# One group of PSUM transposes instead of two, and W1 and W2 in turn for groups 0 to 3, in a causal convolution with a low-rank mixer

## The chip, the core and the metric

The kernel runs on one core of a Trainium2 chip. Its time is the device time of one execution in microseconds (us). The engines are named as in the profile: PE (matrix products; PEld is its weight load), DVE and ACT (both move results out of PSUM), POOL (constants, copies inside SBUF, and the issue of transfers that convert f32 to bf16), SP (issue of other transfers).

## What is computed

Two stages on x of 8 batches, 4224 positions and 192 channels, all in f32 outside:

```python
# stage 1: causal convolution over 7 taps, 8 heads of 24 channels, taps softmaxed per head
w = softmax(weight)                                   # 8 x 7
y[b, s, h, :] = sum_k w[h, k] * x_pad[b, s + k, h, :] # 6 zeros ahead
# stage 2: mixer
h  = y.transpose(0, 2, 1) @ U @ V                     # U: 4224 x 32, V: 32 x 4224, over positions
u  = y + h.transpose(0, 2, 1)
ch = np.maximum(u @ w_ch1, 0.0) @ w_ch2               # 192 x 768 and 768 x 192
out = u + ch
```

h of a position needs the whole batch: first tt = Uᵀy (32 x 192 per batch), then V times tt.

## The kernel before

Positions are cut into tiles of 128: 33 per batch, 264 in all, in 33 groups of eight that run across batches. `manual_schedule` (line 43) means that every engine runs its instructions in the order in which the program writes them; nothing is reordered. Tiles come from pools; PSUM is one pool of eight banks of 512 f32 (line 54), and a new bank waits for the last reader of the tile that had its place.

For a batch the stages are: `conv` or `conv32` (products with a banded matrix made from the taps, evicted from PSUM as y in bf16), `tt_mm` (the products with U), `tt_split` (the sum as a high part by ACT and a low part, the difference, by DVE), `tt_sum` or `tt_done` (sum over four partial rows into tt_sb). For a group: `h_group` (V times tt, eight products, line 457, and additions on DVE that give u, line 479), `transp` (u transposed by a DMA from SP, line 498, as uT), `w1` (36 products in six row blocks of two banks each, line 554; each bank is evicted with relu by ACT or DVE, lines 568 and 570, chosen by a pattern such as "AD"), `w2` (four pairs of tiles, 12 products each, line 583; DVE adds u, line 592, and SP stores, line 600).

**The start.** x of batch 0 comes in three pieces (`KP`, line 86): 20 tiles, then 7, then 6. Line numbers of what happens until W1 starts: constants (109 to 230), warming products on zeros (`idle`, 151 to 161 and 280), the bands (`band_half`, 233), conv of the first piece (690), `u_layout` (694; it brings U, loaded four positions to a row, into tile order with the matrices Eq), U4 by POOL (701), and then the second and third piece with tt between them (735 to 739). The last piece's tt products (`tt_late`) use U4, four copies of U side by side, so that tt_sb follows without a further sum.

Groups 0 and 1 do not take the DMA transpose. `yT_part` multiplies y with the identity so that yᵀ lands in PSUM (line 509), and `hT_part` adds h in the same banks (line 524); ACT and DVE evict the sum as uT. These pieces are interleaved with the end of tt: some transposes run while DVE makes tt_sb.

**The order after that** is written out in `SLOTS` (line 619): a row has the groups of its W1, the groups of its W2, and what is done ahead of which tile pair of W2: "h3" is h and transpose of group 3, "d1" conv of batch 1, "t1" and "s1" its tt, "c2:0:3:AAD" conv of three heads of batch 2 with the eviction pattern AAD, "x2:6" copies on POOL for batch 2, "l2:2" a load of x held back behind the last W2. Groups 0 and 1 have their W1 ahead of both W2; W2 lags W1 by one group until group 3, and from then on three groups of W1 are followed by three of W2. `LOADS` (line 670) holds further loads of x back until a given row block of W1.

**Transfers from POOL** go out in program order, and each waits for the landing of the eighth before it.

Of the kernel before, what the change touches and what calls it, by code (L numbers as in the profile page):

```python
# [7 lines left out]
ALU = mybir.AluOpType  # L8
# [6 lines left out]
def kernel(  # L15
# [10 lines left out]
    nc = tc.nc  # L26
# [59 lines left out]
    KP = [{0: (0, 10), 1: (0, 10)}, {1: (10, NB1 // 2)}, {0: (10, NB0 // 2)}]  # L86
# [21 lines left out]

    dif = cst.tile([P, BW], F32, name="dif")
# [3 lines left out]
    fp = cst.tile([P, P], I32, name="fp")  # L113
    nc.gpsimd.iota(fp[:], pattern=[[1, P]], base=P, channel_multiplier=-1)
    efp = cst.tile([P, 4, P], F32, name="efp")
    iota(efp[:], [[-1, 4], [1, P]], 0, -4)
# [15 lines left out]
    V0_sb = cst.tile([R, 2 * GT * P], BF16, name="V0_sb")  # L132
    nc.gpsimd.dma_start(out=V0_sb[:], in_=moe_V[:, 0 : 2 * GT * P])
# [8 lines left out]
    zz = cst.tile([P, P], F32, name="zz")  # L142
    nc.vector.memzero(zz[:])  # L143

    rq = cst.tile([P, 2], F32, name="rq")
    for r in range(4):
        for n, v in enumerate((32.0, -128.0)):
            nc.vector.memset(rq[QB * r : QB * r + QB, n : n + 1], v * r)
    wps = bank()

    def idle(n, w=4):
        for _ in range(n):
            nc.tensor.matmul(  # L153
                out=wps[:, 0 : w * P].rearrange("p (n t) -> p n t", t=P),
                lhsT=zz[:],
                rhs=zz[:].unsqueeze(1).to_broadcast([P, w, P]),
                start=True,
                stop=True,
            )

    idle(4)


# [3 lines left out]
    for hh in range(2):  # L167
        nc.vector.memzero(bands[hh][:])
    x_zero(0, nc.vector)
    nc.vector.tensor_scalar(  # L170
        out=dif[:], in0=dif[:], scalar1=rq[:, 0:1], scalar2=None, op0=ALU.add
# [13 lines left out]
    nc.vector.tensor_tensor(  # L185
        out=hot[:],
        in0=dif[:].unsqueeze(1).to_broadcast([P, KC, BW]),
        in1=tap[:].unsqueeze(2).to_broadcast([P, KC, BW]),
        op=ALU.is_equal,
    )  # L190
    ident = cst.tile([P, P], BF16, name="ident")
    nc.vector.tensor_scalar(
        out=ident[:], in0=fp[:], scalar1=float(P), scalar2=None, op0=ALU.is_equal
# [15 lines left out]
    for hh in range(2):  # L209
# [10 lines left out]
    Eq = cst.tile([P, 4, P], BF16, name="Eq")  # L220
    nc.vector.tensor_scalar(
        out=Eq[:], in0=efp[:], scalar1=rq[:, 1:2], scalar2=None, op0=ALU.is_equal
    )

    nc.vector.tensor_scalar(
        out=fp[:], in0=fp[:], scalar1=R - 1, scalar2=None, op0=ALU.bitwise_and
    )
    R4 = cst.tile([P, P], BF16, name="R4")
    nc.vector.tensor_scalar(
        out=R4[:], in0=fp[:], scalar1=0.0, scalar2=None, op0=ALU.is_equal  # L230
    )

    def band_half(hh):
# [9 lines left out]
        for r in range(4):  # L243
            o = QB * (r % 2)
            evac(
                "AD"[hh],
                bands[hh][QB * r : QB * r + QB, :, o : o + BW],
                bp[QB * r : QB * r + QB, 0 : HQ * BW].rearrange("p (h t) -> p h t", h=HQ),
            )
# [10 lines left out]
    def u_layout(up):  # L260
        nb = [nfull + (1 if 32 * jj < nlast else 0) for jj in range(4)]
        for a in range(4):
            for jj in range(4):
                nc.tensor.matmul(
                    out=up[jj][:, 0 : nb[jj] * R],
                    lhsT=Eq[32 * jj : 32 * jj + 32, a, :],
# [11 lines left out]

    band_half(0)
    idle(1, 2)  # L280
    band_half(1)


# [112 lines left out]
    def tt_mm(b, js, p=None):  # L396
# [3 lines left out]
        for n, j in enumerate(js):  # L400
# [102 lines left out]
    def yT_part(g, parts):  # L503


        for c, i0, i1, p, _ in parts:
            for i in range(i0, i1):
                for hf in range(2):
                    nc.tensor.matmul(  # L509
                        out=p[HB * hf : HB * hf + HB, (i - i0) * P : (i - i0 + 1) * P],  # L510
                        lhsT=yt[0][:, GT * g + 4 * hf + i, HB * c : HB * c + HB],
                        rhs=ident[:],
                        start=(i == i0),
                        stop=False,
                        tile_position=(0, HB * hf),
                    )

    def hT_part(g, parts):

        uTt[g] = uts.tile([P, 4, 3, P], BF16, name="uT")  # L520
        for c, i0, i1, p, _ in parts:
            for hf in range(2):
                t0 = (2 * g + hf) * 4 * P
                nc.tensor.matmul(  # L524
                    out=p[HB * hf : HB * hf + HB, 0 : (i1 - i0) * P],
                    lhsT=ttb[0][0:R, HB * c : HB * c + HB],
                    rhs=V0_sb[:, t0 + i0 * P : t0 + i1 * P],
# [4 lines left out]
        for c, i0, i1, p, eng in parts:  # L532
            evac(
                eng,
                uTt[g][:, i0:i1, c, :],
                p[:, 0 : (i1 - i0) * P].rearrange("p (i t) -> p i t", t=P),
            )

    RELU = ["AD", "AD", "AA", "AD", "AD", "AD"]
    RELU0 = ["AA", "AD", "AA", "AD", "AA", "AD"]  # L540
# [34 lines left out]
    done_w2 = []  # L575

    def w2(g, t0, n):
# [3 lines left out]
        for a in range(n):  # L581
            for m in range(MC):
                last = nc.tensor.matmul(  # L583
# [6 lines left out]
        done_w2.append(last)  # L590
# [19 lines left out]
    def x_load(b, q, after):  # L610
        if q == 0:
# [8 lines left out]
        ([0], [], {}),  # L620
        ([1], [0], {0: ["h0"], 1: ["h3", "l2:2"], 2: ["l2:3"]}),
        ([2], [1], {0: ["d1", "h1"], 1: ["t1"], 3: ["s1"], 4: ["h4", "x2:6"]}),
        ([3], [2], {1: ["h5"], 3: ["h6"]}),
        (
            [4, 5],
            [3, 4, 5],
            {
                0: ["h7"],
                2: ["c2:0:3:AAD"],
                3: ["c2:3:3:AAD"],  # L630
                4: ["c2:6:2:A", "x3:4"],
                6: ["t2"],
                8: ["s2"],
                9: ["h8"],
# [213 lines left out]
```

## Time and profile before

| what | value |
|---|---|
| three timed runs | 324.85, 325.0, 325.37 us; median 325.0 |
| span of the profiled execution, first to last instruction | 323.2 us |
| PE / DVE / ACT / POOL busy, share of the span | 98% / 83% / 53% / 44% |
| granted TensorE clock in all forty slices | 0.9 or more of full speed |
| chain of work that ended last | PE 92%, ACT 3%, DMA 2%, DVE 1% |
| W2 products (L583), W1 products (L554), of that chain | 42%, 39% |
| first conv product after its x landed / first W1 product | 9.63 us / 20.45 us |
| W1 of groups 2, 3, 4, 6 starts | 33.76, 47.12, 56.34, 81.09 us |
| mean share of time that the 16 DMA engines are busy, q1 and q0 | 45%, 39% |

The page gives the busy time of each engine, the span in forty slices of 8.1 us, and the chain that ended last, followed back from the end. Times inside the execution count from its first instruction. The profile has one execution; what a timed run has beyond the span is the difference of 1.8 us between the median and the span.

### The profile page before, as it was taken

The numbers are of one execution on the slowest core, as the hardware profiler recorded it, in microseconds if no ns is written. First come the engines' busy times: TensorE is split into PE (matmuls) and PEld (weight loads), VectorE is DVE, ScalarE is ACT, GpSimd is POOL, SyncE is SP. The second block draws the span as 40 slices with busy tenths as digits, with TensorE's granted clock in tenths as the row PEclk, the third lists the DMA queues.
The fourth block names the chain that finished last, engine by engine and source line by source line (L and its number), as shares of the span: only waits on it lengthen the run. The fifth ranks groups of instructions, "written<-read, shape, count | busy, mean of one in ns | idle before, by whom it ended". The sixth has DMA issues, their size and how long they took to land.

```text
span 323.2 us, 9583 instructions
## 1 busy us (share of the span) xinstructions
PE 317.6 (98%) x3996; PEld 223.7 (69%) x3996; DVE 268.6 (83%) x551; ACT 170.0 (53%) x344; POOL 142.7 (44%) x111
## 2 busy tenths in 40 slices
PE   8999999999999999999999999999999999999995
PEld 3747676478677647866864884687797497487495
DVE  6769989987977986997898699789888897896863
ACT  1766724860874397088239609824903902912910
POOL 8764179728957983992897497000000000000000
PEclk9999999999999999999999999999999999999999
DMA  9999993999998999599499957138268059048035
GB/s 106 192 191 183 206 209 100 196 192 257 208 135 200 246 142 190 166 189 209 130 237 192 181 149 194 52 105 231 61 178 262 3 150 275 18 121 271 2 121 173
DMA packets 122906, 53.51 MB, mean 166 GB/s; under 512 B 87760, under 2 KB 122832, under 8 KB 122864
## 3 DMA queue, kind: packets, MB, share of 16 engines
q1 hardware_dynamic: 84528, 38.08, 45.4%
q0 software_dynamic: 38192, 14.73, 39.2%
q8 instruction: 31, 0.51, 0.7%
q10 hardware_dynamic: 144, 0.10, 0.1%
q14 instruction: 11, 0.09, 0.1%
HBM read 29.49 MB, written 25.95 MB: 172 GB/s over the span
## 4 chain that ended last, share of the span: by engine, by line
PE 92%; ACT 3%; DMA 2%; DVE 1%; issue 0%; POOL 0%; POOLq 0%
PE ps L583 42%; PE ps L554 39%; PE ps L339 3%; PE ps L457 3%; DMA x_sb<-in_x_dram 2%; PE ps L402 2%; ACT rl_sb L568 2%; PE ps L369 1%; ACT y_sb L256 1%; PE ps L509 1%; DVE u_sb L479 1%; DVE rl_sb L570 1%; PE ps L524 0%; PE ps L428 0%; POOL x_sb L79 0%
## 5 line engine op out<-in xcount | busy, mean ns | idle before, releaser
L568 ACT ACTIVATE rl_sb<-ps 128x512 bf16<-128x512 f32 x233 | 124.3, 604 | 108.0 <-PE ps L554 96.0
L583 PE MATMUL ps<-W_sb,rl_sb 128*128 128x192 bf16 x1584 | 141.2, 246 | 0.2
L583 PEld LDWEIGHTS <-rl_sb 128*128 128x128 bf16 x1584 | 128.3, 98 | 11.8 <-issue 11.5
L554 PE MATMUL ps<-uT,W_sb 64*128 64x512 bf16 x1188 | 131.7, 376 | 0.0
L570 DVE TENSOR_SCALAR rl_sb<-ps 128x512 bf16<-128x512 f32 x163 | 105.3, 688 | 15.7 <-PE ps L554 15.4
L554 PEld LDWEIGHTS <-W_sb 64*128 64x128 bf16 x1188 | 66.9, 94 | 60.4 <-issue 3.9
L592 DVE TENSOR_TENSOR out_sb<-ps,u_sb 128x384 f32<-128x384 f32 (+1 forms) x133 | 70.4, 551 | 25.5 <-PE ps L583 25.0
L305 POOL COPY xb_sb<-x_sb 32x3072 bf16<-32x3072 bf16 (+1 forms) x24 | 67.4, 2824 | 0.5
L479 DVE TENSOR_TENSOR u_sb<-y_sb,ps 128x192 bf16<-128x192 bf16 (+1 forms) x168 | 66.3, 461 | 0.0
L293 POOL COPY xb_sb<-x_sb 128x3072 bf16<-128x3072 bf16 x12 | 32.7, 2742 | 42.1 <-PE ps L339 32.2
L256 ACT ACTIVATE y_sb<-ps 128x384 bf16<-128x384 f32 (+4 forms) x90 | 38.3, 520 | 9.7 <-PE ps L339 7.4
L79 POOL DMA_DIRECT2D x_sb<-in_x_dram x32 | 27.0, 848 | 9.6 <-PE ps L457 3.8
L258 DVE CAST y_sb<-ps 128x408 bf16<-128x408 f32 (+4 forms) x36 | 19.1, 578 | 1.3 <-PE ps L369 1.0
L457 PE MATMUL ps<-tt_sb,V_sb 32*128 32x192 bf16 x264 | 12.4, 246 | 0.1
L339 PE MATMUL ps<-x_sb,band 64*32 64x384 bf16 x192 | 12.1, 333 | 0.0
L339 PE MATMUL ps<-xb_sb,band 64*32 64x384 bf16 x192 | 12.1, 332 | 0.0
L457 PEld LDWEIGHTS <-V_sb 32*128 32x128 bf16 x264 | 4.7, 92 | 7.3 <-issue 7.3
L416 ACT ACTIVATE tt_hi<-ps 128x192 bf16<-128x192 f32 x8 | 2.6, 330 | 11.9 <-PE ps L402 11.9
L369 PE MATMUL ps<-x_sb,band 64*64 64x240 bf16 (+3 forms) x192 | 8.0, 276 | 0.2 <-DMA x_sb<-in_x_dram 0.2
L339 PEld LDWEIGHTS <-band 64*32 64x32 bf16 x384 | 4.5, 89 | 5.2 <-issue 2.4
L153 PE MATMUL ps<-zz 128*128 128x512 f32 (+1 forms) x10 | 6.7, 816 | 1.1 <-DVE zz L143 1.1
L369 PEld LDWEIGHTS <-band 64*64 64x64 bf16 x192 | 6.0, 106 | 2.1 <-issue 1.4
(65 smaller groups left out, 71.3 us busy)
## 6 DMA issues: line engine op xcount, KB each, us to landing
out_dram<-out_sb SPq DMA_DIRECT2D x131, 192.0 KB, 2.7
x_sb<-in_x_dram POOLq DMA_DIRECT2D x14, 384.0 KB, 6.9
x_sb<-in_x_dram POOLq DMA_DIRECT2D x7, 432.0 KB, 6.7
x_sb<-in_x_dram POOLq DMA_DIRECT2D x7, 408.0 KB, 8.0
x_sb<-in_x_dram POOLq DMA_DIRECT2D x1, 504.0 KB, 7.3
uT<-u_sb SPq DMA_TRANSPOSE x31, 3.5
x_sb<-in_x_dram POOLq DMA_DIRECT2D x1, 480.0 KB, 5.6
W_sb<-in_moe_w_ch_dram POOLq DMA_DIRECT2D x2, 192.0 KB, 7.8
```

Of the source, the lines that this page charges most:

```text
L79: return nc.gpsimd.dma_start(out=xt[b][HB * r : HB * r + HB, s0:s1, :], in_=x[b, blk * HB : (blk + s1 - s0) * HB, :].rearrange("(j p) d -> ...
L256: nc.scalar.activation(out=out, in_=in_, func=ACT.Copy)
L293: nc.gpsimd.tensor_copy(out=xbt[b][:, s0:s1, :], in_=xt[b][:, s0 + 1 : s1 + 1, :])
L305: nc.gpsimd.tensor_copy(out=xbt[b][q, s0:s1, :], in_=xt[b][q, s0:s1, :])
L339: nc.tensor.matmul(out=pp[r][QB * cg : QB * cg + QB, 0 : nk[r] * GS], lhsT=w[hr], rhs=t[hr, st : st + 2 * nk[r] - 1 : 2, hs], start=True, ...
L457: nc.tensor.matmul(out=banks[pr][:, a * D : (a + 1) * D], lhsT=V_sb[32 * q : 32 * q + 32, (j // 8) * 2 + j % 2, :], rhs=ttb[b][32 * q : 32 ...
L479: nc.vector.tensor_tensor(out=u_group(g)[:, i : i + n, :, hf, :], in0=yt[b][:, run[0] : run[0] + n, :].rearrange("p n (c k) -> p n c k", c=3),
L554: last = nc.tensor.matmul(out=pps[m][hf][:], lhsT=W1_sb[HB * hf : HB * hf + HB, c, m * P : (m + 1) * P], rhs=uTt[g][HB * hf : HB * hf + HB ...
L568: nc.scalar.activation(out=rl[:, m, hf, :], in_=pp[hf][:], func=ACT.Relu)
L570: nc.vector.tensor_scalar_max(out=rl[:, m, hf, :], in0=pp[hf][:], scalar1=0.0)
L583: last = nc.tensor.matmul(out=cps[:, a * D : (a + 1) * D], lhsT=rlt[g][:, m, hf, (i + a) * P : (i + a + 1) * P], rhs=W2_sb[:, m, :], start ...
L592: nc.vector.tensor_tensor(out=o[:, 0:n, :].rearrange("p n (c k) -> p n c k", c=3), in0=cps[:, 0 : n * D].rearrange("p (n c k) -> p n c k", ...
```

## The change

- The first piece of batch 0 has 19 tiles, the third 7.
- Constants: hot is made in one operation with the shift that dif had before; Eq is one strip of 132 columns of which windows are used, instead of four matrices; R4 and Eq are made after the bands; fp is the first of POOL's constants and efp is gone.
- Three warming products instead of five, issued after the memsets; none between the bands. Each half of the bands is evicted by ACT and DVE together.
- V goes out on POOL ahead of W1; the extra copy of V's first columns (V0) has one group instead of two.
- All conv evictions of the first piece use "AD". U4 is made by DVE in one copy.
- Only group 0 takes its transposes through PSUM: 24 products of line 509 instead of 48, and 6 of line 524 instead of 16. tt of the first piece stands ahead of conv of the second. Group 1 has its h and its DMA transpose ahead of W1 of group 0.
- W1 and W2 alternate for groups 0 to 3. The things done between W2's tile pairs move with it. The loads of x of batch 2 wait for row blocks 2 to 5 of W1 of group 1.

```diff
-    KP = [{0: (0, 10), 1: (0, 10)}, {1: (10, NB1 // 2)}, {0: (10, NB0 // 2)}]
+    KP = [{0: (0, 9), 1: (0, 10)}, {1: (10, NB1 // 2)}, {0: (9, NB0 // 2)}]
...
-    V0_sb = cst.tile([R, 2 * GT * P], BF16, name="V0_sb")
+    V0_sb = cst.tile([R, GT * P], BF16, name="V0_sb")
...
+    for q in range(4):
+        src = moe_V[:, 0 : full * 8 * P].rearrange("r (k q t) -> r k q t", q=4, t=2 * P)
+        nc.gpsimd.dma_start(
...
-    idle(4)
+    for w in (4, 4, 4):
+        idle(w)
...
-    nc.vector.tensor_tensor(
+    nc.vector.scalar_tensor_tensor(
         out=hot[:],
...
-    band_half(0)
-    idle(1, 2)
-    band_half(1)
+    band_half(0, "AAAD")
+    band_half(1, "AADD")
+    nc.vector.tensor_scalar(out=fp[:], ...)
+    nc.vector.tensor_scalar(out=R4[:], ...)
+    nc.vector.tensor_scalar(out=Eq[:, 3 : 3 + P].rearrange("p (k a) -> p k a", a=4)[:, :, 0], ...)
...
+    def hT(g, ps):
...
+            k = 2 if c == 0 else 4
+            for n in range(4 // k):
+                evac("AD"[n], ...)
-    RELU0 = ["AA", "AD", "AA", "AD", "AA", "AD"]
+    RELUS = {0: ["AA", "AD", "AD", "AD", "AD", "AD"], 1: ["AA", "AA", "AD", "AD", "AD", "AD"]}
...
     SLOTS = [
-        ([0], [], {}),
-        ([1], [0], {0: ["h0"], 1: ["h3", "l2:2"], 2: ["l2:3"]}),
-        ([2], [1], {0: ["d1", "h1"], 1: ["t1"], 3: ["s1"], 4: ["h4", "x2:6"]}),
-        ([3], [2], {1: ["h5"], 3: ["h6"]}),
+        ([0], [0], {0: ["h0"], 2: ["h2"]}),
+        ([1], [1], {1: ["h3"]}),
+        ([2], [2], {0: ["d1"], 1: ["t1"], 3: ["s1"], 4: ["h4", "x2:6"]}),
+        ([3], [3], {0: ["h5"], 2: ["h6"], 4: ["h7"]}),
         (
             [4, 5],
-            [3, 4, 5],
-            {0: ["h7"], 2: ["c2:0:3:AAD"], 3: ["c2:3:3:AAD"], 4: ["c2:6:2:A", "x3:4"],
-             6: ["t2"], 8: ["s2"], 9: ["h8"], 11: ["h9"]},
+            [4, 5],
+            {1: ["c2:0:3:AAD"], 2: ["c2:3:3:AAD"], 3: ["c2:6:2:A", "x3:4"],
+             4: ["t2"], 6: ["s2"], 7: ["h8"], 8: ["h9"]},
         ),
     ]
-    LOADS = {2: [(1, 5), (1, 5)], ...}
+    LOADS = {2: [(1, 2), (1, 3), (1, 4), (1, 5)], ...}
...
     for h in range(0, H, 2):
-        conv(0, h, 2, [0, 1], "AA" if h == 0 else "AD", KP[0])
+        conv(0, h, 2, [0, 1], "AD", KP[0])
     work = [bank() for _ in range(4)]
     tp = bank()
+    y0 = [bank() for _ in range(3)]
     u_layout(work)
+    nc.vector.tensor_copy(out=U4_sb[:], ...)
...
-    yT_part(0, parts0)
...
-    conv_piece(1)
-    tt_mm(0, piece_tiles(0) + piece_tiles(1), tp)
-    tt_split(0, tp)
-    conv_piece(2)
-    ps0 = work[3]
+    for c in range(2):
+        yT(0, c, y0[c])
+    tt_mm(0, early, tp, 0, na)
+    for n, h in enumerate(range(0, H, 3)):
+        conv(0, h, min(3, H - h), [1], "DAD"[n], KP[1], {1: work[n]})
+    yT(0, 2, y0[2])
+    for n, h in enumerate(range(0, H, 3)):
+        conv(0, h, min(3, H - h), [0], "ADA"[n], KP[2], {0: work[(3, 0, 1)[n]]})
+        if n == 0:
+            tt_mm(0, early, tp, na)
+            tt_split(0, tp)
+    ps0 = tp[:, 256 : 256 + D]
...
-    yT_part(0, more[0:1])
     tt_late(ps0)
-    yT_part(0, more[1:])
-    yT_part(1, parts1)
     tt_done(0, ps0)
-    hT_part(0, parts0 + more)
-    yT_part(1, rest)
-    hT_part(1, parts1 + rest)
+    hT(0, y0)
+    h_group(1)
+    transp(1)
```

`yT` and `hT` are `yT_part` and `hT_part` for whole chunks of 64 channels with a bank each; the sum of tt of batch 0 now goes to other columns of the bank that its first part used.

## The prediction

> **What bounds the kernel now.** I read the page's busy shares and its forty slices first, then the chain of waits in order of time, then the timelines of the engines around the places that the change touches. Durations come from the one profiled execution: its span is 323.2 us, 1.8 us under the median of 325.0 of the three timed runs (324.85 to 325.37). I take that 1.8 us as what lies around the span and as unchanged, so a shift worked out inside the span moves the median by as much. About 0.2% (0.65 us) is what a measurement of this kernel can tell from no change.
>
> ```profile
> PE 317.6 (98%) x3996; PEld 223.7 (69%) x3996; DVE 268.6 (83%) x551; ACT 170.0 (53%) x344; POOL 142.7 (44%) x111
> ...
> PE   8999999999999999999999999999999999999995
> ```
>
> The matrix engine is busy in every slice, so a gain has to be work taken from it, or a stall. The chain says where stalls are:
>
> ```profile
> 9.63 1.98 PE ps L369 x62
> ...
> 18.35 0.83 PE ps L524 x10
> 19.18 0.57 PE ps L509 x16
> 19.75 0.76 PE ps L524 x6
> 20.51 1.23 PE ps L554 x10
> 21.74 3.04 ACT rl_sb L568 x6
> ...
> 81.16 11.84 PE ps L554 x108
> ```
>
> From 81.16 us (W1 of groups 6 to 8) on the chain is PE work in blocks, and both kernels give it the same instructions in the same order. So the whole effect is the shift of that start. Ahead of it the chain holds front work (conv, U, tt, transposes), and from 20.5 us W1 with ACT and DVE behind it.
>
> **Front, up to the h products of group 0 (L524, at 18.34).** The change takes 24 of 48 PSUM transposes and 10 of 16 h products, nearly all in the stretch of 19.11 to 20.44, 1.33 us. That is its possible gain. What it puts in the way is on DVE:
>
> ```profile
> 9.25 1.30 DVE L258 CAST band<-ps 32x152 bf16<-32x152 f32 x4
> 10.68 1.79 DVE L258 CAST y_sb<-ps 128x480 bf16<-128x480 f32 x3
> 12.38 0.75 DVE L258 CAST U_sb<-ps 128x256 bf16<-128x256 f32 x2
> ```
>
> 1. Bands. PE finishes the second half at about 9.15 in both (it waits for DVE's product of taps). The fused form of hot is not in the trace: between 0.43, the row of the plain form in the same shape, which leaves the bands where they are, and 0.43 + 0.85 with the add that it takes in, which would put them 0.5 late. I take 0.43. Now ACT copies two quarters and DVE two, but DVE's first waits for ACT's second (same tile): 4 x 0.31 from 9.15 gives 10.39, against 10.55 now. The gain is 0.16.
> 2. The three small constants (fp, R4, Eq) stand behind the bands: 0.26 and 0.23 as in the rows at 8.81 and 9.11, and some 0.12 for Eq on 32 columns. DVE reaches the y evictions at about 10.95 (now 10.68).
> 3. It has four instead of three of them ("AD" for every pair): 0.57 apart (three in 1.79, the last 0.65 long), so U's first can start at 10.95 + 4 x 0.57 = 13.22 and its second ends at 13.97 (now 13.13).
> 4. The tt products now stand ahead of the second conv piece, and the fourth of them needs that U eviction: 14.01. Sixteen more at 0.083 per four, a gap of 0.17 (as at 15.0), and conv piece 1 starts at 14.5; now it starts at 13.0, on the landing of its x. So PE is 1.5 late there. Its cover was that conv needs no U.
> 5. Piece 1 takes 1.15, the last 8 transposes 0.35 with their gaps; piece 2 starts at 16.14, its first eviction on ACT at 16.80 (0.66 after the start, as 13.66 after 13.00). ACT's tt_hi comes 0.48 later (17.28 to 17.61), DVE's tt_lo 17.64 to 18.0 (0.33 and 0.36 in the rows), and DVE's y eviction of heads 3 to 5 stands behind tt_lo: 17.95 to 18.63 (0.68). Seven late tt products (six now) at 0.082 plus 0.24 for the last end at 19.40, tt_sb 0.36: the h products start at 19.82. Now 18.34, so 1.48 late.
> 6. From there: three pairs of h products at 0.21, h of group 1 (8 x L457, 0.3), ACT's evictions of the three chunks (0.28, 0.48, 0.59, 0.09 for the signals) to 21.56. The second row block of W1 waits for the third chunk, so its first finished bank comes at about 22.6. Now 21.74. The first 1.48 has shrunk to 0.9: of the 1.33 removed, 0.57 is realized, the rest goes into waiting for evictions that the second group's transposes covered. **W1 of group 0 ends 0.9 late.**
>
> DVE's four additions for group 1 (1.94) fall beside that wait; two of them release the banks of W1's third block at 21.5, before 22.5. U4 on DVE instead of POOL: 0.82 there for 768 elements, on DVE not shown for 896; between 0.2 (the 0.23 of R4's 128) and 1.2 (one f32 512-column pass at 0.69, scaled). It runs from 13.9 and its neighbour is ready at 15.1, so it costs nothing at either end. POOL's freed time goes to DMA issue.
>
> **Transfers.** The first x of batch 0 lands 48 KB sooner (0.26 at the 504 KB per 2.69 us between 6.90 and 9.59); step 4 does not wait for x any more. V's four transfers now go ahead of W1's. Landings follow one another: V's at 21.3 to 22.4 are 0.36 apart, W1's four take 3.8 after V0 (15.1 to 18.9). Second x piece 14.5, half of V0 0.33, V 1.44, W1 3.8: W1 is in at about 20.1. Each POOL issue also waits for the landing of the eighth before it (W1's last waits for V0, 14.8); issued at 15.4 with 5.4 (the least of V's times) it lands at 20.8. Blocks 2 to 5 of W1 are wanted from 22.5, V from 20.4 (lands 16.3), W2 from 25.6 (lands about 23.6). Nothing, with 1.7 to spare at the tightest. x of batch 2 now waits for W1 of group 1 instead of W2 (issue at 32 to 34, now 29.3 to 32.7); POOL's shift copies take 17 after it and end near 59 as now (59.9), wanted at 70. Nothing. Transpose of group 1 by DMA: first in SP's queue behind the tap weights, issued at 22.6, 5.1 as the first one at 27.14, so 27.7; wanted after 30. Nothing.
>
> **W1 and W2 in turn.** Now W1 of group 1 stands between W1 of group 0 and its W2, so relu is always done. In the new order W2's first tile needs the last relu on ACT. After group 0, h0 stands between (0.3) and the wait is 0.2; after group 1 ACT has 8 relus 0.476 apart and ends 0.9 after PE, of which five products cover 0.42: 0.5. After group 3 h5 covers it. Against that the present 0.23 stall of W1 of group 1 (4.16 for 3.93) and a little more go: **+0.25**. h of group 1 is gone from behind conv of batch 1 (40.92 to 41.49 now): **-0.4**. h7's additions move from behind W1 of groups 4 and 5 to ahead of it; an h ahead of W1 costs 0.4 for group 3 (4.34 at 47.12), and 0.3 of that is there already by h6: **+0.15**.
>
> **Conv of batch 2.** It stays with three blocks of heads, but there is one W2 tile pair between the last block and the tt products, where there were two.
>
> ```profile
> 67.30 1.68 ACT L256 ACTIVATE y_sb<-ps 128x384 bf16<-128x384 f32 x4 [2.27 <-PE ps L339]
> 69.32 3.42 ACT L256 ACTIVATE y_sb<-ps 128x384 bf16<-128x384 f32 x8 [0.34 <-PE ps L339]
> 74.14 0.33 ACT L416 ACTIVATE tt_hi<-ps 128x192 bf16<-128x192 f32 x1 [1.41 <-PE ps L402]
> ```
>
> ACT needs 12 evictions at 0.43, 5.2, from 0.42 after the first product: 5.7 to 5.8. PE now has 4 x 1.05 + 1.7 = 5.9 there and takes 6.31; with one tile pair less it has 4.85 and would wait. The whole stretch from W1's end at 64.5 to 81.09 becomes 12.8 for 16.59, where the work taken out is 4.15 + 0.28: **+0.6**. Bounds: 0, if the 0.4 of stall that DVE's h7 additions make at 65.2 goes too, and 0.9.
>
> Sum: 0.9 + 0.25 - 0.4 + 0.15 + 0.6 = +1.5 on 325.0: **326.5 us**.
>
> **A rule that speaks against the change.** The warming products now start at about 2.15, behind DVE's memsets, instead of 1.07, and are three, not five. In the trace their passes come 0.85 apart until 5.5 and 0.43 after that. From 2.15, the same 4.4 ends at 6.6, before the bands at 7.35 and conv at 9.4. The Trainium skill ("TensorE: Matmul & The Clock Gate", Part 1) says that the gate opens after one busy window of some 3.4 us, that this window runs free of the kernel's start, and that an idle window closes it. By that rule it could open a window later, about 10, and the sum would be nearer 327.4 than 326.5.
>
> **Rivals.**
> - *DVE is not late in the front* (faster). For it: DVE's 83% is mostly later, and steps 1 to 3 hang on short copies at one place. Against it: four evictions at 0.57 are rows. It decides at the h products: the sum is zero if they start at 18.3, and a gain that shows begins below 17.7. The floor: x of piece 2 lands at 14.46, then conv 1.2, eviction 0.65, late tt 0.8, tt_sb 0.4, gives 17.5: 2.3 earlier than I have, -0.8: 324.2. If conv of batch 2 does not wait either, 323.6.
> - *Half of it* (no change): the h products at about 18.6 or no stall in batch 2's conv: 324.4 to 325.6.
> - *Cold products or late weights* (slower still): if the passes are still 0.85 apart when conv starts, its 16 steps of 0.1025 doubled are 1.6, less the 0.6 that evictions cover, so +1.0, 327.5; W1's last weights landing after 22.5 cost what they are late, 1 or more: 327.5 to 328.
> - That the change does not do what it says can be left out for the counts (the program order shows them); whether the transposes were on the path is the question of step 6.
>
> **Chances.** Forecast (325.65 to 327.4) 0.46, cold or late 0.14, half of it 0.20, DVE not late 0.20. So faster 0.20, within 0.2% 0.20, slower 0.60. The range reaches down into the first rival and up to the last: 323.9 to 327.8.
>
> **What would show it.** Conv piece 1 starting at 14 or later, with DVE's U evictions ahead of it, shows steps 1 to 4; tt_lo ahead of a y eviction and h products near 19.8 step 5; first relu at 22.6 step 6; a wait of 0.4 to 0.9 ahead of batch 2's tt products the last term. I am wrong if h products start before 18.3, if W1 waits for weights, or if W1 of groups 6 to 8 starts before 81.1.

## The result and the profile after

The changed kernel took 337.4 to 341.1 us, the kernel before 324.85 to 325.4: a ratio of 1.043, with a 95% interval of 1.0375 to 1.049. The forecast was 326.5 us with a range of 323.9 to 327.8. The direction was right. The size was wrong by 13 us. Slow runs, over 1.5% above the fastest run of the same kernel, are left out of all totals here: 345.5 us of the changed kernel, one each of e2 and h2 below, two of the four of f2 (337.8 and 338.8 us, so that f2 has no interval), and the profiled execution of e4, of which only the first part is read.

The profiled execution took 339.34 us (span 337.6). All times below are of profiled executions unless a run's total is meant. Busy shares and slices on the page of the changed kernel:

```profile
PE 321.7 (95%) x3958; PEld 221.0 (65%) x3958; DVE 270.1 (80%) x548; ACT 169.2 (50%) x340; POOL 141.4 (42%) x109
...
PE   5888899999996999999999999999999999999995
...
PEclk9989799999998999999999999999999999999999
...
PE 78%; DMA 9%; DVE 6%; POOL 5%; issue 1%; ACT 1%; POOLq 0%; DVEq 0%
```

The kernel before had PE at 98% and at 9 in every slice but the first and last. Now slices 1 to 5 are thin, slice 13 (101 to 110 us) is a 6, and the granted clock of the matrix engine dips in slices 3, 5 and 13. The chain has lost 14 points of PE to DMA, DVE and POOL.

Where the time goes can be read from the starts and lengths of W1. The third kernel is experiment e3 below: the kernel before with only the new order.

| us | before | order alone (e3) | changed |
|---|---|---|---|
| W1 of group 1: start / length | other order | 29.32 / 4.06 | 34.97 / 5.75 |
| W1 of groups 4, 5 | 56.34 / 8.24 | 61.24 / 8.80 | 68.38 / 8.80 |
| W1 of groups 6 to 8 | 81.09 / 11.90 | 82.23 / 13.01 | 89.37 / 13.01 |
| W1 of groups 9 to 11, start | 109.39 | 111.64 | 123.41 |
| start of the last W2 block | 307.73 | 311.38 | 321.75 |

The shift of 14.0 is complete at W1 of group 9 and has four parts. **7.1** is the distance to the order-alone kernel at W1 of group 6 (89.37 less 82.23), all of it there already at W1 of group 1 (5.65 in its start, 1.69 in its length); experiment e2 below splits it into 4.4 for the DMA transpose of group 1 and 2.8 for the front. **1.1** is the order by itself up to there (82.23 less 81.09). **1.1** is the longer W1 of groups 6 to 8. **4.6** is lost between its end and group 9 (21.03 us against 16.40), in the conv of batch 3.

The first part, in the chain of the changed kernel (start, length, what):

```profile
18.28 0.36 DVE tt_lo L426
...
18.64 0.60 DVE y_sb L252
...
20.49 0.42 PE ps L531 x2
...
21.82 1.83 PE ps L562 x8
23.65 11.27 DMA uT<-u_sb
34.92 0.05 issue
34.97 5.79 PE ps L562 x36
```

Up to the h products the front came as worked out, with tt_lo ahead of a y eviction. They start at 20.49 (19.82 forecast). The first large error is the line at 23.65: the transpose of group 1 was put at 5.1 us and landed 11.27 us after its issue, while three loads of x of batch 1 were in flight. W2 of group 0 was done at 32.6 and PE stood until 34.97.

The last part, in the timeline of PE (start, length, form; in brackets the idle time ahead and who ended it):

```profile
104.40 0.33 PE L348 MATMUL ps<-xb_sb,band 64*32 64x384 bf16 x1
107.53 0.33 PE L348 MATMUL ps<-xb_sb,band 64*32 64x408 bf16 x1 [2.80 <-POOL xb_sb L314]
...
108.50 2.10 PE L589 MATMUL ps<-W_sb,rl_sb 128*128 128x192 bf16 x12
```

The first block of conv of batch 3 took 4.17 us instead of 0.71, because POOL's copies were not done, and the W2 pair after it ran at half speed (2.10 us instead of 1.16; the granted clock is 0.5 from 107.7 to 111.1). POOL's timeline shows where the copies were late. First the kernel before, then the changed one; L305 and L314 are the same copies, L79 issues the loads of x of batch 3:

```profile
41.20 2.74 POOL L293 COPY xb_sb<-x_sb 128x3072 bf16<-128x3072 bf16 x1 [7.65 <-DMA x_sb<-in_x_dram]
...
60.11 1.63 POOL L79 DMA_DIRECT2D x_sb<-in_x_dram  x2
...
88.32 3.08 POOL L305 COPY xb_sb<-x_sb 32x3456 bf16<-32x3456 bf16 x1
```

```profile
51.56 2.74 POOL L302 COPY xb_sb<-x_sb 128x3072 bf16<-128x3072 bf16 x1 [9.13 <-DMA x_sb<-in_x_dram]
...
59.52 11.24 POOL L314 COPY xb_sb<-x_sb 32x3072 bf16<-32x3072 bf16 x4
...
70.94 0.82 POOL L79 DMA_DIRECT2D x_sb<-in_x_dram  x1
...
76.83 0.88 POOL L79 DMA_DIRECT2D x_sb<-in_x_dram  x1 [1.10 <-PE ps L562]
...
104.40 3.08 POOL L314 COPY xb_sb<-x_sb 32x3456 bf16<-32x3456 bf16 x1
```

The first copy for batch 2 is 10.4 late, the first load of batch 3 10.8 late, and the last copy for batch 3 ends at 107.5 instead of 91.4, 16.1 late. In the kernel before conv of batch 3 began at 95.0, so it had 3.6 us of slack; PE itself is 9.4 late at this place. 16.1 less 9.4 less 3.6 is the stall, 3.1.

### The profile page after: what moved, and what is told of

The parts are those of the page before. It is cut to its first block, busy times and chain, and to the rows that moved or that the text cites. A ratio compares the mean times of both kernels' runs of the same rounds, so it can differ in the third digit from the quotient of the medians.

```text
span 337.6 us, 9503 instructions
## 1 busy us (share of the span) xinstructions
PE 321.7 (95%) x3958; PEld 221.0 (65%) x3958; DVE 270.1 (80%) x548; ACT 169.2 (50%) x340; POOL 141.4 (42%) x109
## 4 chain that ended last, share of the span: by engine, by line
PE 78%; DMA 9%; DVE 6%; POOL 5%; issue 1%; ACT 1%; POOLq 0%; DVEq 0%
PE ps L589 35%; PE ps L562 34%; DMA x_sb<-in_x_dram 4%; DMA uT<-u_sb 3%; POOL xb_sb L314 3%; PE ps L348 3%; PE ps L466 2%; PE ps L378 2%; PE ps L411 2%; DVE u_sb L488 2%; DMA w_sb<-in_weight_dram 1%; DVE y_sb L252 1%; POOL xb_sb L302 1%; DVE rl_sb L578 1%; DVE pr L219 1%
## 5 line engine op out<-in xcount | busy, mean ns | idle before, releaser
L562 PE MATMUL ps<-uT,W_sb 64*128 64x512 bf16 x1188 | 136.5, 383 | 3.0 <-DMA uT<-u_sb 2.4
L562 PEld LDWEIGHTS <-W_sb 64*128 64x128 bf16 x1188 | 65.5, 95 | 69.5 <-issue 9.5
L314 POOL COPY xb_sb<-x_sb 32x3072 bf16<-32x3072 bf16 (+1 forms) x24 | 67.4, 2824 | 0.5
L250 ACT ACTIVATE y_sb<-ps 128x384 bf16<-128x384 f32 (+4 forms) x88 | 37.4, 519 | 14.5 <-PE ps L348 10.7
L79 POOL DMA_DIRECT2D x_sb<-in_x_dram x32 | 27.1, 851 | 20.8 <-PE ps L562 19.5
L252 DVE CAST y_sb<-ps 128x408 bf16<-128x408 f32 (+4 forms) x38 | 20.3, 580 | 4.0 <-PE ps L348 3.4
L348 PE MATMUL ps<-xb_sb,band 64*32 64x384 bf16 (+1 forms) x192 | 13.0, 346 | 2.8 <-POOL xb_sb L314 2.8
L466 PE MATMUL ps<-tt_sb,V_sb 32*128 32x192 bf16 x264 | 12.6, 247 | 0.2 <-DVE u_sb L488 0.2
L348 PE MATMUL ps<-x_sb,band 64*32 64x384 bf16 x192 | 12.6, 347 | 0.0
L378 PE MATMUL ps<-x_sb,band 64*64 64x168 bf16 (+3 forms) x192 | 8.4, 276 | 0.2 <-DVE band L252 0.2
L411 PE MATMUL ps<-y_sb,U_sb 128*32 128x192 bf16 x257 | 7.8, 248 | 0.3
```

What stands on the lines that cost most here:

```text
L79: return nc.gpsimd.dma_start(out=xt[b][HB * r : HB * r + HB, s0:s1, :], in_=x[b, blk * HB : (blk + s1 - s0) * HB, :].rearrange("(j p) d -> ...
L250: nc.scalar.activation(out=out, in_=in_, func=ACT.Copy)
L314: nc.gpsimd.tensor_copy(out=xbt[b][q, s0:s1, :], in_=xt[b][q, s0:s1, :])
L348: nc.tensor.matmul(out=pp[r][QB * cg : QB * cg + QB, 0 : nk[r] * GS], lhsT=w[hr], rhs=t[hr, st : st + 2 * nk[r] - 1 : 2, hs], start=True, ...
L466: nc.tensor.matmul(out=banks[pr][:, a * D : (a + 1) * D], lhsT=V_sb[32 * q : 32 * q + 32, (j // 8) * 2 + j % 2, :], rhs=ttb[b][32 * q : 32 ...
L562: last = nc.tensor.matmul(out=pps[m][hf][:], lhsT=W1_sb[HB * hf : HB * hf + HB, c, m * P : (m + 1) * P], rhs=uTt[g][HB * hf : HB * hf + HB ...
```

## The experiments

Totals are given as medians or as the span of the runs; the ratios are to the kernel before (325.0 us). Theory T, at the start, was: the transposes and loads of the start are late, and the lateness passes through x of batch 2, POOL's copies and x of batch 3. Its rival R: the front's lateness, relu hand-offs and slow products.

**e1: x of batch 1 behind the transpose.**

```diff
-    transp(1)
+    first = transp(1)
-        x_part(1, *xp)
+        held(x_part(1, *xp), first)
```

> The changed kernel with one edit: the second, third and fourth x load of batch 1 are held back until the transpose of group 1 has landed (in the changed kernel they were issued 3 to 5 us ahead of it and the transpose took 11.27 us, against 5.12 for the first one of the kernel before). Theory T (transfers: the transpose is late because those loads are in flight, and the lateness goes on to x of batch 2, POOL's copies and the conv of batch 3): the transpose takes 5 to 6 us and lands near 29, PE's wait of 2.39 us ahead of W1 of group 1 goes and with it the slow products of that W1 (5.75 us, about 1.7 too many); x of batch 2 is issued about 4 us sooner, so the 5.7 us that conv of batch 3 loses shrinks by up to 4. Time 332 to 336 us. Rival R (the front's lateness, the relu hand-offs and slow products make the loss, and the transpose only fills a gap that is there anyway): 339 us or more, with the same gap ahead of W1 of group 1 ended by something else.

Measured: 338.8 to 342.6 us, ratio 1.0485 (1.043 to 1.054). T was right on the transpose and wrong on the time. The issues of 22 to 24 us (operation, count, median us to landing), and then those of 31 to 32, in the transfers of e1:

```profile
uT<-u_sb SPq DMA_TRANSPOSE x1, 4.8
```

```profile
uT<-u_sb SPq DMA_TRANSPOSE x1, 11.5
```

Without the loads group 1's transpose takes 4.76 us and its W1 runs at once, in 4.06. But the held loads now meet the transpose of group 2, which takes 11.47, and x of batch 2 lands at 59.2 instead of 56.1. PE's waits in e1:

```profile
PE ps L562 <- DMA uT<-u_sb: 3.2, 1, 3.2
PE ps L348 <- POOL xb_sb L314: 3.1, 1, 3.1
```

Same two waits, the first one group further on. The loads delay a transpose, which is T's mechanism; that taking one transpose out of their way gains something is refuted.

**e2: group 1 through PSUM again.** After `tt_late`, three calls `yT(1, c, y1[c])`; `hT(1, y1)` instead of `transp(1)`; `V0_sb` for two groups.

> The changed kernel with group 1 again transposed through PSUM (24 products with the identity and 6 with V's columns more, no DMA transpose of group 1; order, front and held loads stay). Theory T: the wait of 2.39 us and the slow W1 of group 1 go (-4.1), the 30 products and their evictions come back (+1.3 to +2), x of batch 2 comes some 2 us sooner and takes up to that off the loss at the conv of batch 3: 334 to 338 us. Rival R (front, hand-offs): no gain, as the products are added to a front that is late already: 341 us or more.

Measured: 332.7 to 336.9 us, ratio 1.027 (1.023 to 1.031). W1 of group 1 starts at 32.1 and takes 4.06; W1 of group 6 starts at 85.0 (89.4 with the DMA transpose). So the step to the DMA transpose costs 4.4 us, PSUM products included. The other 2.8 of the 7.1 above (85.0 less 82.2 of e3) stay with the changed front. The wait for POOL is still there (3.3 at conv of batch 3): without any DMA transpose of group 1, the copies for batch 2 still end at 69.4, 9.5 later than in the kernel before.

**e3: the order alone.** The kernel before with `SLOTS`, `RELUS` and `LOADS` of the changed one, and like that one without the hold that kept the transpose of group 3 until conv of batch 1 was done.

> The kernel before with only the order of the changed kernel: W1 and W2 in turn for groups 0 to 3, its relu patterns, the loads of x of batch 2 behind row blocks 2 to 5 of W1 of group 1; front, constants, and both groups through PSUM as before. Theory T: the loads of x of batch 2 are issued at 30 to 33 us, about as before (29.3 to 32.7), so POOL's copies end near 60 and conv of batch 3 waits for nothing: 325 to 327 us (the hand-offs and the conv of batch 2 cost +0.6 by the prediction's terms). Rival R with the order as cause (relu hand-offs in each of eight turns, conv of batch 2): 330 us or more. Conv of batch 3 waiting for POOL here too would say that the order alone makes the POOL chain late.

Measured: 329.3 to 330.1 us, ratio 1.014 (1.013 to 1.016), between the two. The table above has its starts: 1.1 up to W1 of group 6, 1.1 inside it, 1.4 waiting for POOL at conv of batch 4 (1.95 us for its first block instead of 0.54). The 1.1 inside W1 is on DVE, whose timeline has, with W1 begun at 82.23:

```profile
81.09 2.00 DVE L479 TENSOR_TENSOR u_sb<-y_sb,ps 128x192 bf16<-128x192 bf16 x5
83.01 0.55 DVE L592 TENSOR_TENSOR out_sb<-ps,u_sb 128x384 f32<-128x384 f32 x1
83.48 1.94 DVE L479 TENSOR_TENSOR u_sb<-y_sb,ps 128x384 bf16<-128x384 bf16 x4
```

h of groups 8 and 9 now stands in the last two places ahead of W1, and their additions fill DVE until 85.4, while W1's first relus wait. In the kernel before another tile pair stood between.

**e4: the front alone.** The changed front, group 1 through PSUM, the order of before.

> The kernel before with only the front of the changed kernel: constants, three warming products, V ahead of W1, bands by ACT and DVE, pieces of 19, 7 and 7 tiles, tt of the first piece ahead of conv of the second; group 1 still through PSUM and the order of before. Theory T: the front costs what its own steps cost, 1.0 to 1.5 us, and about 1.9 for the slow products of W1 of group 0 if these are slow here too; the loads of x of batch 2 go as before: 326 to 329 us. Rival R with the front as cause: 332 us or more.

Measured: 326.0 to 328.4 us, ratio 1.007 (1.005 to 1.009). W1 of group 0 starts at 21.86, 1.4 late, and takes 4.06. T's range holds; as the cause of 14 us the front is out. This kernel keeps the PSUM products of group 1, which the change takes out.

**f1: x of batch 3 earlier.**

```diff
-        ([2], [2], {... 4: ["h4", "x2:6"]}),
+        ([2], [2], {... 4: ["h4", "x2:2"]}),
-    LOADS = {2: ..., 3: [(4, 1), (4, 4), (5, 1), (5, 4)]}
+    LOADS = {2: ..., 3: [(3, 1), (3, 2), (3, 4), (3, 5)]}
```

> The changed kernel with one edit: the loads of x of batch 3 stand ahead of the last four of POOL's copies for batch 2 (held on row blocks of W1 of group 3), so that they no longer queue behind all of them. In the changed kernel they were issued at 70.9 to 76.8 and landed at 78.3 to 90.9, and conv of batch 3 then waited for POOL's copies (4.17 us for the first three heads instead of 0.71, and the W2 pair after it 2.10 instead of 1.16). Theory P (POOL's chain of load, copies, load sets conv of batch 3; it costs about 4.6 us in the profiled run): loads issued at 60 to 65, copies of batch 3 start when conv of batch 2 is done, near 82, and end near 102, before they are wanted at 104: 334 to 336 us. Rival R (POOL is the bound through its copies alone, 20 us for a batch, or the loads collide with other transfers): 338 us or more, the wait only moves to a later batch.

Measured: 333.8 to 335.5 us, ratio 1.028 (1.024 to 1.033), 5 us less than the changed kernel. POOL in f1:

```profile
59.00 0.83 POOL L79 DMA_DIRECT2D x_sb<-in_x_dram  x1 [1.17 <-PE ps L562]
...
81.48 5.43 POOL L302 COPY xb_sb<-x_sb 128x3072 bf16<-128x3072 bf16 x2 [7.89 <-PE ps L348]
...
97.61 3.08 POOL L314 COPY xb_sb<-x_sb 32x3456 bf16<-32x3456 bf16 x1
```

The copies for batch 3 now wait for PE's conv of batch 2, not for a load, and end at 100.7, before they are wanted at 103.5. Conv takes 0.71 and the W2 pair 1.16 again. Theory P holds, with the size it gave.

**h3: the hold on W1 alone.** The second edit of f1 without the first.

> The changed kernel with one edit: the loads of x of batch 3 are held on row blocks of W1 of group 3 instead of groups 4 and 5, but stay behind POOL's six copies for batch 2 in POOL's own order. Theory Q (the queue binds: POOL issues nothing until its copies are done at 70.8): the four loads go out together at 70.8 to 73.5 instead of 70.9 to 76.8 and land some 3 us sooner at most; conv of batch 3 still waits: 336 to 340 us. Theory H (the hold on W1 of group 4 binds): as in f1, 334 to 336 us, with the loads issued near 60.

Measured: 337.3 to 340.5 us, ratio 1.0415 (1.038 to 1.0455), as the changed kernel. POOL issues nothing before its copies are through:

```profile
59.22 11.24 POOL L314 COPY xb_sb<-x_sb 32x3072 bf16<-32x3072 bf16 x4
...
70.64 3.35 POOL L79 DMA_DIRECT2D x_sb<-in_x_dram  x4
```

Theory Q is right: the queue binds here; with the queue open too (f1) the loads go out 7 to 12 us sooner.

**f4: x of batch 2 earlier.** `LOADS[2]` on blocks 2 to 5 of W1 of group 0.

> The changed kernel with one edit: the loads of x of batch 2 are held on row blocks 2 to 5 of W1 of group 0 instead of group 1, so issued at about 25 to 28 us instead of 38.3 to 41.6. Theory P (lateness of this load goes through POOL's copies to the load of batch 3 and its conv): they land by 45 to 48, the copies end near 61 to 64, x of batch 3 is issued by 65, conv of batch 3 waits for nothing: 334 to 336 us, if the transposes of groups 1 and 2 are not later for it. Rival R (the transfers are a shared resource and already full up to 40 us): the transposes of groups 2 and 3 land later than at 39.5 and 56.4 and PE waits for one of them: 338 us or more.

Measured: 341.7 to 343.3 us, ratio 1.051 (1.047 to 1.056). R was right on the time, and in part on the mechanism: the transpose of group 2 lands later (44.2, after 12.6 us), that of group 3 sooner (52.8), and the one that PE waits for, 4.1 us, is that of group 1 (12.1 us). x of batch 2 is in at 51.6: 4.5 sooner, for an issue 14 sooner. So most of the earlier issue is lost among the transfers that are under way up to 50 us. Conv of batch 3 waits 5.4: the loads of batch 3 are held on W1 of group 4 until 71.7, so this hold binds once the copies are earlier.

**f3: products in the waits.** 16 products of 256 columns between the last conv and W1 of group 0, 20 ahead of W1 of group 1; results unused.

> The changed kernel with products added whose results nobody reads: 16 in the waits of the front between the last conv and W1 of group 0, 20 in the wait ahead of W1 of group 1 (each 256 columns, some 0.11 us). Theory C (the products of W1 of groups 0 and 1 are slow, 6.03 and 5.75 us where 4.06 is usual, because PE stands idle ahead of them): both take about 4.1, and group 1's W1 ends 1.7 sooner; time 336 to 338 us, or less if x of batch 2, which is held on this W1, then comes soon enough for conv of batch 3. Rival R (the slow products come from something else, such as transfers into the same memory): W1 stays at 5.7 to 6.0 us, and the added products cost what does not fit into the waits: 339.5 to 341 us.

Measured: 340.9 to 344.5 us, ratio 1.053 (1.047 to 1.0585). The stretch 18 to 28 us (length, busy time of PE, PEld, DVE, ACT, POOL, then granted clock, DMA share, GB/s), the changed kernel first, then f3:

```profile
18.00:28.00 10.00, 8.87 (x82) 4.14 (x77) 6.37 (x13) 5.73 (x13) 5.31 (x13) 0.83 1.42 165
```

```profile
18.00:28.00 10.00, 9.29 (x101) 5.73 (x99) 8.10 (x17) 4.96 (x11) 5.36 (x13) 1.00 1.40 167
```

The clock stays at 1.00 and W1 of group 0 takes 4.12 instead of 6.03. That fits theory C, but one execution does not show it: of the seven profiled kernels that have this front, group 1 by DMA and no such products, six have a slow W1 of group 0 (5.16 to 6.03) and one has not (4.34, f2). The time does not fall but lies above both theories' ranges (median 342.8), since W1 of group 1 waits for its transpose anyway (landed 37.0, PE idle 4.0, and its W1 at 5.75 again). Where the transpose of group 1 is this late, the slow W1 of group 0 is off the path.

**f2: places of h.** h7 behind W1 of groups 4 and 5; s2, h8 and h9 one pair earlier.

> The changed kernel with two additions of h moved: h of group 7 back behind W1 of groups 4 and 5, h of group 9 from directly ahead of W1 of groups 6 to 8 to one tile pair earlier (h of group 8 and the sum of tt of batch 2 one pair earlier as well). In the order-alone kernel W1 of groups 4 and 5 took 8.80 us (8.24 in the kernel before) and that of groups 6 to 8 13.01 (11.90). Theory D (DVE's four additions of h stand ahead of the first relus of W1): 8.24 and about 11.9 again, 1.0 to 1.7 us less at W1 of group 6; the conv of batch 3 waits for POOL at a set time, so what is won ahead of it is lost there again and the time falls by 0 to 0.5 only: 338.5 to 340.5 us. Rival (PE sets this stretch, POOL's wait follows it): the whole 1.7 shows, 337.5 us.

Measured: 332.6 and 333.6 us, 6 less than the changed kernel. That is more than either theory gave, and not all of it is the places of h. W1 of groups 4 and 5 took 7.94 (8.80), of 6 to 8 12.43 (13.01). In the profiled execution the clock never fell, so that W1 of group 1 took 4.06 and not 5.75, which the edit does not explain. And x of batch 3 landed at 83.8 instead of 90.9: h7's transpose is issued at 75.9, behind those loads, no longer at 72.1 among them. Conv of batch 3 no longer waits for POOL (0.71 for its first block); conv of batch 4 does, for 2.0.

**h2: the order with h in its places.** e3 with f2's edit.

> The order-alone kernel (329.6 us: the kernel before with W1 and W2 in turn) with the places of h of groups 7 and 9 mended and nothing else: no hold of the transpose of group 3, x of batch 3 as there. Theory S: 0.5 to 0.6 us less in each of the two stretches of W1, and the conv of batch 4, which waited 1.4 us for POOL, waits less, since x of batch 3 lands sooner without the transpose of group 7 beside it: 327 to 328.5 us. Rival (POOL's chain sets the time; W1's lengths do not show): 329 us or more. Anything under 326 would say that W1 and W2 in turn cost nothing by themselves.

Measured: 326.0 us (325.8 to 328.4), ratio 1.004 (1.002 to 1.006). W1 of groups 4 and 5:

```profile
60.52 7.95 PE L554 MATMUL ps<-uT,W_sb 64*128 64x512 bf16 x72
```

No wait for POOL is left, and the time lies below theory S's range. Of e3's 4.6 us the two places of h made about 3.5, of which 1.4 is in W1's lengths and 1.4 in the wait at conv of batch 4, for which the transpose of group 7 no longer stands among the loads of batch 3. What stays for W1 and W2 in turn is 1.0 us by the medians (0.6 to 2.0 by the ratio's interval).

**g1, g2, g3: repairs put together.** g1 is the changed kernel with f1, f2 and the transpose of group 3 held behind conv of batch 1; g2 adds e2; g3 is e3 with the three edits of g1.

> The changed kernel with three edits: the loads of x of batch 3 ahead of the last copies for batch 2, h of groups 7 and 9 back to their places (both alone gave 332 to 335 us), and the transpose of group 3 issued only after conv of batch 1, as in the kernel before, so that it does not stand in the loads of x of batch 2. Theory S (a DMA transpose and the loads of x slow each other; what is late goes through POOL's copies to the conv of batch 3): the transpose of group 3 takes 4 to 6 us instead of 11.7, x of batch 2 lands 3 to 5 us sooner, no wait for POOL at all. What stays is group 1's transpose: W1 of group 1 starts 5 to 6 us late, and is slow in some runs (up to 1.7): 330 to 332.5 us. Rival (each repair only moves the loss): 334 us or more.

> The kernel changed and mended as the one before it in this list, and group 1 through PSUM again: what is left of the change is its front, W1 and W2 in turn, and the late place of h of group 1's neighbours. Theory S: W1 of group 1 starts at about 32 (32.1 in the run with that edit alone), nothing waits for POOL, and the time is the kernel before plus the front and the slow W1 of group 0: 326.5 to 328.5 us, 3 to 4 less than with the DMA transpose of group 1. Rival (the order has a cost of its own of some 4 us, as in the order-alone kernel): 330 us or more.

> The kernel before with the changed order, with x of batch 3 loaded ahead of the last copies, h of groups 7 and 9 in their places and the transpose of group 3 held behind conv of batch 1. The order without these three took 329.6 us, 4.6 more than before. Theory S: W1 and W2 in turn cost nothing by themselves, the 4.6 us come from the places of h (0.56 and 1.11 us by the lengths of W1) and from the late loads of x: 325 to 326 us. Rival R (relu hand-offs and conv of batch 2, as the prediction had it): 326.5 us or more.

Measured: 332.9 (ratio 1.023 to 1.026), 330.7 (1.016 to 1.020) and 328.4 us (1.009 to 1.012). No wait for POOL is left in any. g1 keeps group 1's late transpose (11.0 us) and is a little over its range; g2 and g3 miss theirs by 2 and lie where their rivals put them, though not for the rivals' reasons alone. In g3 the hold made a wait of its own: the transpose of group 3 lands at 52.4, when W1 wanted it at 51.2, and that of group 5, now beside the early loads of batch 3, costs another 1.1; with the 1.0 of the order (h2) that is all of its 3.4. In g2 PE waits 0.8 for the transpose of group 3 and 0.7 for a relu; with the 2.8 of the front and the 1.0 of the order that makes 5.3 of its 5.6. Repairs that are right alone collide in the same transfers.

**g4: the disputed cost by itself.** The kernel before with the transpose of group 3 issued at 34.1, among the loads of batch 2.

> The kernel before with one edit: the transpose of group 3 is issued as soon as its u is there, near 31 us, among the four loads of x of batch 2 (issued 29.3 to 32.7), and no longer held until conv of batch 1 is done (41.04). It measures the disputed cost by itself. Theory S (transposes and x loads slow each other): the transpose takes 9 to 12 us instead of 5.60, x of batch 2 lands 2 to 5 us later than 45.30, POOL's copies end at 62 to 65 instead of 59.9, x of batch 3 is issued later, and its conv, for which the copies are just in time at 95.0, waits 2 to 5 us: 327 to 330 us. Rival N (a transfer that is not wanted yet costs nothing): 325.0 us, within 0.6.

Measured: 325.2 us (325.0 to 326.9), ratio 1.0016 (1.0001 to 1.003). The issues of 33 to 35 us:

```profile
x_sb<-in_x_dram POOLq DMA_DIRECT2D x1, 408.0 KB, 13.9
uT<-u_sb SPq DMA_TRANSPOSE x1, 11.8
```

The transpose takes 11.84 instead of 5.60, as S said. The load of batch 2 that lands last does so only 1.5 later, which the slack of 3.6 covers: N is right on the time. So the loads slow a transpose by 6 us; the other direction is shown only for 1.5.

**h1: one place of h in the kernel before.** s1 and h4 one pair earlier.

> The kernel before with one edit: the sum of tt of batch 1 and h of group 4 one tile pair of W2 earlier, so that h of group 4 is no longer directly ahead of W1 of group 3 (which takes 4.41 us there, 4.06 where nothing of h stands ahead of it). Theory D (DVE's additions for h stand ahead of the first relus): W1 of group 3 takes 4.06, and all later work is 0.35 us sooner: 324.6 to 324.8 us. Rival: the 0.35 comes back as a wait for tt_lo or tt_sb, which are then wanted one pair sooner (tt_lo ends at 44.6, when the pair ends): 325.0 us, within 0.2.

Measured: 325.05 us (324.6 to 327.9), ratio 1.000 (0.997 to 1.003). W1 of group 3 took 4.06, but the gain of 0.35 does not show in the total; in the profiled execution a stall of 0.9 at a W2 product, for which the profile gives no releaser, outweighs it. Inconclusive at this spread. No kernel here beats the one before.

## Why the prediction was wrong

**Steps 1 to 5, the front up to the h products: right to 0.7 us.** Conv of the second piece starts at 15.15 (14.5 forecast) with the U evictions ahead of it, tt_lo runs ahead of the last y eviction, the h products start 0.67 later than worked out. In the profiled run the tap weights landed at 4.47 instead of 3.65, and 0.47 of that shows in the bands. The fused hot took 0.49 (0.43 taken). DVE's timeline has the four y evictions and U's two, which end at 14.65 (13.97 forecast, 0.47 of the difference from the weights):

```profile
11.63 2.35 DVE L252 CAST y_sb<-ps 128x480 bf16<-128x480 f32 x4
13.90 0.75 DVE L252 CAST U_sb<-ps 128x256 bf16<-128x256 f32 x2
```

**Step 6, "W1 of group 0 ends 0.9 late": mis-sized.** Its products start 1.4 late, its first relu is at 23.79 (22.6 forecast), and it ends 3.3 late, because its products took 6.03 instead of 4.06. Later the front costs 2.8 us at W1 of group 6 (e2 against e3) and 2.2 in e4 (1.5 to 3.0), both with group 1's products in PSUM; by the forecast's own terms such a front would cost 1.5 (0.9 and the 0.57 that it counts as won).

**"Transpose of group 1 by DMA: ... 5.1 as the first one at 27.14 ... Nothing": the step that failed first.** The row of 5.12 came from a transpose issued when the loads of batch 1 were nearly through (the last landed 3.8 us later). The new one is issued 3.5 to 5.2 us after three loads with 1.2 MB. Measured: 11.27 us, landed 34.92 instead of 27.7. With those loads moved away it takes 4.76 (e1). It costs 4.4 us against PSUM (e2). Often the transpose lands about when the last load issued ahead of it does: 34.92 beside 35.38 here, 43.02 beside 43.75 in e1, 45.95 beside 46.77 in g4; but 34.03 beside 36.94 in f1. I took the duration of a row and left out what was in flight beside it.

**"x of batch 2 ... copies end near 59 as now ... wanted at 70. Nothing": the second failure.** They ended at 70.8. The late transpose, which moves the hold on W1 of group 1, is the smaller part of it: the copies end at 63.9 in e3 (the order alone) and at 69.4 in e2 (the order and the front, group 1 through PSUM). So 4.0 of the 10.8 come with the order, 5.5 with the front and 1.3 with the transpose of group 1. With the order the last of the loads is issued 1.6 later and lands 4.0 later; the change also drops the hold of the transpose of group 3, which the forecast does not price and which makes 1.5 of this by itself (g4). And the step looked at one consumer only. POOL's next instructions in order are the loads of x of batch 3, and the conv of batch 3 had 3.6 us of slack against a lateness that grew to 16.1 and PE's own 9.4. f1 shows it: 5 us back for issuing these loads 7 to 12 us sooner.

**"h7 ahead of W1 ... +0.15": mis-sized, and half missing.** The place of h7 costs 0.56 (8.80 for 8.24; 0.85 against the 7.95 of h2) and that of h9, which I did not follow, 1.11 (13.01 for 11.90), besides putting a transpose among the loads of batch 3. Mending both is worth about 3.5 us in the order-alone kernel (h2).

**"W1 and W2 in turn": small, as forecast.** +0.25 and -0.4, and +0.6 for conv of batch 2, make 0.45 beside a measured 1.0 (0.6 to 2.0) for the whole order with h in its places.

**Conv of batch 2, +0.6: nothing.** The stretch from W1's end to W1 of group 6 took 12.19 us, against 12.8 worked out and 12.16 for its work alone (16.59 less 4.15 and 0.28). From the first conv product (78.21) to the first tt product (83.50) it is 5.29, where I had 5.7 to 5.8 for ACT's twelve evictions. ACT runs them without a gap, as forecast, but from 0.42 after the first product they take 5.22 with the last one's latency, which overlaps the tt products:

```profile
78.63 5.22 ACT L250 ACTIVATE y_sb<-ps 128x384 bf16<-128x384 f32 x12 [1.00 <-PE ps L348]
84.52 0.33 ACT L425 ACTIVATE tt_hi<-ps 128x192 bf16<-128x192 f32 x1 [0.66 <-PE ps L411]
```

**The rule on the clock.** The forecast weighed the slow products for the start of conv. Conv was not slow, and W1 of groups 0 and 1 was. The clock of 0.83 above is a mean; in shorter stretches of the changed kernel (columns as in f3):

```profile
19.00:22.40 3.40, 2.45 (x27) 1.16 (x28) 1.64 (x5) 1.36 (x4) 3.24 (x8) 1.00 1.22 127
22.40:25.90 3.50, 3.50 (x19) 1.57 (x19) 1.94 (x5) 1.98 (x4) 1.07 (x5) 0.51 1.54 181
25.90:29.30 3.40, 3.40 (x40) 2.14 (x37) 3.37 (x6) 1.98 (x4) 0.00 (x0) 1.00 1.54 180
...
36.00:39.50 3.50, 3.50 (x22) 1.28 (x18) 0.92 (x2) 2.75 (x6) 0.83 (x1) 0.51 0.72 192
107.70:111.20 3.50, 3.50 (x57) 2.07 (x43) 1.60 (x3) 1.75 (x5) 1.42 (x2) 0.51 1.35 185
```

So the clock is at half for 3.4 us, three times: at W1 of group 0, at W1 of group 1 (1.69 of the loss) and at conv of batch 3 and the W2 pair behind it. The Trainium skill ("TensorE: Matmul & The Clock Gate", Part 1) names an idle window of some 3.4 us for the clock to fall. The length agrees with these rows. But ahead of the first fall there was no idle window: PE was busy 2.45 of the 3.4 us before it, with no gap over 0.5 us. By an idle window alone the clock would not have fallen there. What share of busy time is enough no run settles: in e1 PE waited 3.1 us for conv of batch 3 and the clock stayed at 1.00.

**A transfer's turn.** The Trainium skill ("DMA: Bandwidth & Descriptors", Queues, rings and completion order) says that a DMA engine goes round its queues packet by packet. By that a transpose would take turns with loads issued before it and be through in about twice its own time, 10 us from 5.1 as an estimate; 11.0 to 14.2 us were measured for that of group 1 in seven kernels with loads beside it. Had I applied the rule, group 1 would have been at about 33 and not at 27.7. That it often lands with the last load issued before it looks like one common queue, but in f4 the transpose of group 2, issued at 31.56 after four loads (24.5 to 27.0), landed at 44.16, ahead of three of them (45.2, 48.2, 51.6). A transpose can pass earlier loads, which speaks for turns; how large its share of them is no run shows.

What stays open: the rate. In the stretch 18 to 28 us the changed kernel moved 165 GB/s and the kernel before 190; W2's weights landed 1.8 us later than in the kernel before and the pieces of x of batch 1 2.1 to 4.7 later. The forecast had W2's weights at 23.6; they came at 26.17. Behind the slow W1 of group 0 this did not show in the changed kernel; in f1, f2 and f3 W2 of group 0 waited 0.6 to 1.4 us for them. No run isolates why.

## What to carry to other kernels

A transfer's time in a row holds for the company it had there: before a hidden transfer is priced at nothing, list what is in flight on the same engines when it will be issued, and what it will delay in turn. Follow a late load through every instruction that stands behind it in the issuing engine's order, to the second and third consumer, and compare the lateness with the slack of each. Where an order is rewritten, look at what stands directly ahead of each long block: four additions on another engine cost as much there as a stall.

## What was not expected of the hardware

- A DMA transpose of one group takes 3.2 to 5.6 us with little or nearly finished loads beside it, and 7 to 14 us when 1 MB or more of loads was issued in the 3 to 7 us before it.
- The TensorE clock fell to half for 3.4 us after a stretch of that length in which PE was 72% busy and no gap was over 0.5 us. After an idle time of 2.3 to 4.7 us W1 took 5.7 to 6.6 instead of 4.06 in seven kernels, but in one with 2.8 us of idle time it took 4.06 (f2).
- A wait of 2.1 to 3.3 us of PE for POOL cost almost another us in the changed kernel, e2, f3 and h3: the W2 pair after it took 2.10 instead of 1.16. After 3.1 us in e1 it did not (1.16).
